# Attention and a gated two-layer network on one core: the row sums of two heads are inverted together, one head later

## The chip, the cores and the metric

One core of a Trainium2 chip. The metric is the device time of one execution in microseconds (us). Five engines work side by side, each through its own queue in order: TensorE (PE; its weight loads are listed as PEld), VectorE (DVE), ScalarE (ACT), GpSimd (POOL) and SyncE (SP), which issues most of the transfers.

## The reference

```
scores = scale * q @ k^T            # B=4, H=8, S=768, D=64
keep   = (pos_k < n_sink) | (0 <= pos_q - pos_k < window)     # 4 and 128
scores = where(keep, scores, -1e9);  scores -= rowmax
a      = exp(scores);  a = a / (sum(a) + 1e-9)
attn   = a @ v                      # then heads side by side: x is 3072 x 512
h      = x @ w_in                   # 512 x 2048
g      = max(h, 0) + log1p(exp(-|h|))
out    = g @ w_out                  # 2048 x 512
```

## The kernel before

**Tiling.** The 3072 rows are cut into 12 chunks of 256 rows, three to a batch. A chunk has 8 heads. Because of the window, a block of 128 query rows needs only its own block of keys, the block before it, and 8 keys at the start of the sequence (the sinks). So a head of a chunk is two row blocks (`j` = 0, 1) of 128 rows, each with 136 weights: 128 that hold the two key blocks folded into one square, and 8 for the sinks. From the third chunk on, products are made of a high and a low part of each number, to keep the precision; the first two chunks (`exact`) use float32 directly.

**The way of one head.** Each part is a method of `_Attention`, and a letter in the tables of `_fast`:
- `scores` (S): TensorE makes `s` in PSUM.
- `softmax` (T): VectorE folds the square and takes the row extremum (L243, L249, which also writes the negative of the scores to `a`); ScalarE takes the exponential in place and sums each row into the small tile `sm` (L250).
- `normalise` (N): VectorE adds 1e-9 to the two sums (L256) and inverts them into `rc` (L257); then the 128 weights of each row block are multiplied by it (L262 on ScalarE, L264 on VectorE or GpSimd). The string `NM` says which engine does it for the first 17 heads; for all others it is GpSimd.
- `sink_weights` and `sink` (k, K): the sinks' weights of four heads at once are multiplied by `rc` on VectorE (L269), transposed and split.
- `weights_t` (W): TensorE transposes the weights into `t` (L297); ScalarE copies them to `th`, VectorE makes the rest `tl`; GpSimd masks both into `pt` with four instructions, two of `th` and two of `tl` (L308, L311).
- `values` (V): TensorE multiplies the sinks' values (L327) and then `pt` (L333) into `x`. `out` (O) moves `x` to `xf` and splits it into `xh` (ScalarE) and `xl` (GpSimd, for the last head of a chunk VectorE).

Beside it runs the network of the chunk before (`_Moe`): `up` (U, L459), `softplus` (F, L466 to L468 on ScalarE), `gate` and `residue` (P, R: L474, `gh`, and the subtraction `gl` on VectorE), `down` (D, E: L496 to L498).

**What sets the order.** TensorE's and SyncE's instructions stand in the order in which the program calls these parts. Up to the third chunk that is the string `START`, written by hand, in which the conversion of the weights (a, c, d, l) is mixed in. From there on each step of a loop runs the letters of `STEADY` once; scores, softmax and normalise work four heads ahead of the transposition. One step per head, eight steps per chunk, and the first step of a chunk has an order of its own. At the start of a batch GpSimd also builds the sinks' values of the batch (`sinks`, L151 to L159), half of them ahead of head 6 of the chunk before. VectorE, ScalarE and GpSimd take what they are given in the order that the framework makes of the same calls, and each works through it in order.

Of the kernel before, what the change touches and what calls it, by code (L numbers as in the profile page):

```python
# [11 lines left out]
F32 = mybir.dt.float32  # L12
# [5 lines left out]
AF = mybir.ActivationFunctionType  # L18
ALU = mybir.AluOpType

B, H, S, D = 4, 8, 768, 64
DM, DFF = 512, 2048
P = 128
# [3 lines left out]
CH = 2  # L27
# [10 lines left out]
G = 4  # L38
# [24 lines left out]
def _turn(engines, k):  # L63

    return engines[min(k, len(engines) - 1)]
# [57 lines left out]
class _Attention:  # L123
# [110 lines left out]
    def softmax(self, h):  # L234
        c, nc, chunk = self.c, self.c.nc, self.chunk
        g, hh = h // G, h % G
        if hh == 0:
            self.a[g] = c.ap.tile([P, G, CH, KW], F32, tag="a", name=f"a{chunk}_{g}")
            self.rc[g] = c.sp.tile([P, CH, G], F32, tag="rc", name=f"rc{chunk}_{g}")
        sm = c.sp.tile([P, CH], F32, tag="sm", name=f"sm{chunk}_{h}")  # L240
        self.sm[h] = sm
        for j in range(CH):
            nc.vector.copy_predicated(self.s[h, j][:, :P], c.diag[:], self.s[h, j][:, KW:])  # L243
        for j in range(CH):
            a = self.a[g][:, hh, j]
            k = (chunk * H + h) * CH + j
            nm = c.stats[:, k : k + 1]
            m = c.masks[min(self.i0 + j, 2)]
            nc.vector.tensor_tensor_reduce(a, self.s.pop((h, j))[:, :KW], m[:], -SCALE, BIG, ALU.add, ALU.min, nm)  # L249
            nc.scalar.activation(a, a, AF.Exp, bias=nm, scale=-1.0, accum_out=sm[:, j : j + 1])  # L250

    def normalise(self, h):
        c, nc = self.c, self.c.nc
        g, hh = h // G, h % G
        rc, sm = self.rc[g][:, :, hh], self.sm.pop(h)
        nc.vector.tensor_scalar(sm[:], sm[:], 1e-9, None, ALU.add)  # L256
        nc.vector.reciprocal(rc, sm[:])  # L257
        for j in range(CH):
            a = self.a[g][:, hh, j, :P]
            eng = _turn(c.NM, self.chunk * H + h)  # L260
            if eng == "A":
                nc.scalar.mul(a, a, rc[:, j : j + 1])  # L262
            else:
                (nc.vector if eng == "V" else nc.gpsimd).tensor_scalar(a, a, rc[:, j : j + 1], 0.0, ALU.mult, ALU.add)  # L264

    def sink_weights(self, g):
        c, nc, chunk = self.c, self.c.nc, self.chunk
# [639 lines left out]
```

## Time and profile before

| | us |
|---|---|
| median of 3 runs | 729.31 (729.26 to 729.64) |
| the profiled execution, its own time | 731.77 |
| its span, first to last instruction | 730.1 |
| TensorE busy | 701.6 |
| VectorE busy | 579.6 |
| ScalarE busy | 452.2 |
| GpSimd busy | 377.5 |

A row of a timeline gives the start in us from the beginning of the span, the duration, the engine, the line, the instruction, what it writes and reads, and the shape; in brackets stand the idle time of the engine ahead of it and what ended it. A row of the waits gives who waited for whom, the sum, how often, and the longest.

### The profile page before, as it was taken

The numbers are of one execution on the slowest core, as the hardware profiler recorded it, in microseconds if no ns is written. First come the engines' busy times: TensorE is split into PE (matmuls) and PEld (weight loads), VectorE is DVE, ScalarE is ACT, GpSimd is POOL, SyncE is SP. The second block draws the span as 40 slices with busy tenths as digits, with TensorE's granted clock in tenths as the row PEclk, the third lists the DMA queues.
The fourth block names the chain that finished last, engine by engine and source line by source line (L and its number), as shares of the span: only waits on it lengthen the run. The fifth ranks groups of instructions, "written<-read, shape, count | busy, mean of one in ns | idle before, by whom it ended". The sixth has DMA issues, their size and how long they took to land.

```text
span 730.1 us, 13819 instructions
## 1 busy us (share of the span) xinstructions
PE 701.6 (96%) x4505; PEld 622.6 (85%) x4505; DVE 579.6 (79%) x1693; ACT 452.2 (62%) x1104; POOL 377.5 (52%) x682
## 2 busy tenths in 40 slices
PE   7789999999999999999999999999999999999996
PEld 5467789988898998989899898898898898998995
DVE  6799988878988888887987987988898887864332
ACT  4579856666765766665666666665766666654331
POOL 5666486565564554664554564556555465552000
PEclk9899999999999999999999999999999999999998
DMA  9886622211411321321222222221212222100001
GB/s 308 268 316 216 182 67 74 73 53 38 118 49 48 110 64 49 106 64 46 84 64 67 77 79 68 78 76 45 86 51 79 69 76 78 58 14 1 29 1 34
DMA packets 40875, 63.21 MB, mean 87 GB/s; under 512 B 4634, under 2 KB 22362, under 8 KB 40794
## 3 DMA queue, kind: packets, MB, share of 16 engines
q1 hardware_dynamic: 40506, 61.97, 27.9%
q8 instruction: 38, 0.62, 0.4%
q14 instruction: 43, 0.35, 0.2%
q10 hardware_dynamic: 288, 0.26, 0.1%
HBM read 55.93 MB, written 6.29 MB: 85 GB/s over the span
## 4 chain that ended last, share of the span: by engine, by line
PE 73%; DVE 8%; ACT 7%; POOL 7%; issue 4%; DMA 1%; POOLq 0%; ACTq 0%
PE h L459 30%; PE acc L498 10%; PE acc L496 9%; PE acc L497 9%; PE x L333 6%; PE t L297 2%; POOL pt L308 2%; PE s L230 2%; PE s L231 2%; PE x L327 2%; POOL pt L311 2%; ACT a L250 1%; ACT mt L466 1%; ACT mt L467 1%; POOL vs L159 1%
## 5 line engine op out<-in xcount | busy, mean ns | idle before, releaser
L459 PE MATMUL h<-xh,wi 128*128 128x256 f32 x1536 | 253.6, 287 | 0.0
L459 PEld LDWEIGHTS h<-xh,wi 128*128 128x128 f32 x1536 | 211.1, 191 | 1.6 <-issue 0.5
L264 POOL TENSOR_SCALAR a<-a,rc 128x128 f32<-128x128 f32 x178 | 69.2, 401 | 186.1 <-DVE rc L257 150.4
L459 PE MATMUL h<-xl,wi 128*128 128x256 f32 x768 | 154.5, 283 | 0.0
L496 PE MATMUL acc<-wo,gh 128*128 128x512 f32 x384 | 151.7, 395 | 0.0
L498 PE MATMUL acc<-wo,gl 128*128 128x512 f32 x384 | 150.9, 393 | 0.6 <-DVE gl L56 0.6
L497 PE MATMUL acc<-wo,gh 128*128 128x512 f32 x384 | 150.6, 392 | 0.0
L459 PEld LDWEIGHTS h<-xl,wi 128*128 128x128 f32 x768 | 119.6, 192 | 0.0
L474 DVE SCALAR_TENSOR_TENSOR mt<-h,mt 128x512 f32<-128x512 f32 x96 | 66.1, 688 | 66.8 <-ACT mt L468 58.4
L466 ACT ACTIVATE mt<-h 128x512 f32<-128x512 f32 x96 | 57.1, 595 | 96.0 <-PE h L459 96.0
L250 ACT ACTIVATE a<-a,stats 128x136 f32<-128x136 f32 x192 | 76.3, 398 | 56.9 <-DVE stats L249 56.3
L498 PEld LDWEIGHTS acc<-wo,gl 128*128 128x128 f32 x384 | 72.1, 188 | 17.5 <-DVE gl L56 1.0
L496 PEld LDWEIGHTS acc<-wo,gh 128*128 128x128 f32 x384 | 72.1, 188 | 12.8 <-issue 0.3
L497 PEld LDWEIGHTS acc<-wo,gh 128*128 128x128 f32 x384 | 72.2, 188 | 9.0
L56 DVE TENSOR_TENSOR gl<-mt,gh 128x512 fp32r<-128x512 f32 x96 | 74.8, 780 | 0.3
L308 POOL TENSOR_SCALAR_AFFINE_SELECT pt<-tl 128x256 fp32r<-128x256 f32 x80 | 59.7, 746 | 27.8 <-DVE tl L56 27.7
L308 POOL TENSOR_SCALAR_AFFINE_SELECT pt<-th 128x256 fp32r<-128x256 f32 (+1 forms) x96 | 42.5, 442 | 40.2 <-ACT th L48 36.7
L467 ACT ACTIVATE mt<-mt 128x512 f32<-128x512 f32 x96 | 60.7, 633 | 3.1
L468 ACT ACTIVATE mt<-mt 128x512 f32<-128x512 f32 x96 | 60.7, 632 | 3.0
L48 ACT CAST qkh<-qk 128x656 fp32r<-128x656 f32 x80 | 59.5, 744 | 0.9 <-DMA qk<-qk 0.9
L333 PE MATMUL x<-pt,vv 128*128 128x256 f32 (+1 forms) x216 | 48.7, 328 | 8.0 <-POOL pt L311 8.0
L56 DVE TENSOR_TENSOR kl<-qk,qkh 128x400 fp32r<-128x400 f32 x80 | 53.6, 670 | 2.5
(185 smaller groups left out, 1234.7 us busy)
## 6 DMA issues: line engine op xcount, KB each, us to landing
qk<-qk SPq DMA_DIRECT2D x160, 164.0 KB, 3.1
vr<-v SPq DMA_DIRECT2D x32, 192.0 KB, 2.8
out<-o SPq DMA_DIRECT2D x24, 256.0 KB, 2.2
vr<-v SPq DMA_DIRECT2D x16, 128.0 KB, 2.3
q<-q SPq DMA_DIRECT2D x7, 256.0 KB, 5.1
k<-k SPq DMA_DIRECT2D x8, 200.0 KB, 4.1
wi00r<-w SPq DMA_DIRECT2D x1, 511.8 KB
wi01r<-w SPq DMA_DIRECT2D x1, 511.8 KB, 6.3
```

The lines of the kernel that those rows point to most:

```text
L56: (nc.vector if eng == "V" else nc.gpsimd).tensor_tensor(out, a, b, ALU.subtract)
L250: nc.scalar.activation(a, a, AF.Exp, bias=nm, scale=-1.0, accum_out=sm[:, j : j + 1])
L264: (nc.vector if eng == "V" else nc.gpsimd).tensor_scalar(a, a, rc[:, j : j + 1], 0.0, ALU.mult, ALU.add)
L308: nc.gpsimd.affine_select(pt[:, e, :, 1], src[:], [[0, CH], [1, P]], ALU.is_ge, 0.0, base=0, channel_multiplier=-1)
L333: nc.tensor.matmul(x[:, :, o], w, pt[:, :, m], start=False, stop=n == 2, skip_group_check=True)
L459: nc.tensor.matmul(h[:, j], wt, x, start=k == 0, stop=k >= len(prods) - 2, skip_group_check=True)
L466: nc.scalar.activation(t[:], h[:], AF.Abs)
L467: nc.scalar.activation(t[:], t[:], AF.Exp, scale=-1.0)
L474: nc.vector.scalar_tensor_tensor(t[:], h[:], 0.0, t[:], ALU.max, ALU.add)
L496: nc.tensor.matmul(acc[:], gh[:, j, q], wh, start=f == 0, stop=False, skip_group_check=True)
L497: nc.tensor.matmul(acc[:], gh[:, j, q], wl, start=False, stop=False, skip_group_check=True)
L498: nc.tensor.matmul(acc[:], gl[:, j, q], wh, start=False, stop=f == 2 * FP - 1, skip_group_check=True)
```

## The change

`softmax` gives the two heads of a pair one tile of sums with four columns. `normalise` returns at once for an even head. For an odd head it adds 1e-9 to all four sums, inverts them with one instruction, and then issues the multiplications of both heads, the even one's first.

```diff
--- before.py
+++ after.py
@@ -237,8 +237,9 @@
         if hh == 0:
             self.a[g] = c.ap.tile([P, G, CH, KW], F32, tag="a", name=f"a{chunk}_{g}")
             self.rc[g] = c.sp.tile([P, CH, G], F32, tag="rc", name=f"rc{chunk}_{g}")
-        sm = c.sp.tile([P, CH], F32, tag="sm", name=f"sm{chunk}_{h}")
-        self.sm[h] = sm
+        if h % 2 == 0:
+            self.sums = c.sp.tile([P, CH, 2], F32, tag="sm", name=f"sm{chunk}_{h}")
+        self.sm[h] = sm = self.sums
         for j in range(CH):
             nc.vector.copy_predicated(self.s[h, j][:, :P], c.diag[:], self.s[h, j][:, KW:])
         for j in range(CH):
@@ -247,21 +248,26 @@
             nm = c.stats[:, k : k + 1]
             m = c.masks[min(self.i0 + j, 2)]
             nc.vector.tensor_tensor_reduce(a, self.s.pop((h, j))[:, :KW], m[:], -SCALE, BIG, ALU.add, ALU.min, nm)
-            nc.scalar.activation(a, a, AF.Exp, bias=nm, scale=-1.0, accum_out=sm[:, j : j + 1])
+            nc.scalar.activation(a, a, AF.Exp, bias=nm, scale=-1.0, accum_out=sm[:, j, h % 2 : h % 2 + 1])
 
     def normalise(self, h):
+
+        if h % 2 == 0:
+            return
         c, nc = self.c, self.c.nc
         g, hh = h // G, h % G
-        rc, sm = self.rc[g][:, :, hh], self.sm.pop(h)
+        rc, sm = self.rc[g], self.sm.pop(h)
+        assert self.sm.pop(h - 1) is sm
         nc.vector.tensor_scalar(sm[:], sm[:], 1e-9, None, ALU.add)
-        nc.vector.reciprocal(rc, sm[:])
-        for j in range(CH):
-            a = self.a[g][:, hh, j, :P]
-            eng = _turn(c.NM, self.chunk * H + h)
-            if eng == "A":
-                nc.scalar.mul(a, a, rc[:, j : j + 1])
-            else:
-                (nc.vector if eng == "V" else nc.gpsimd).tensor_scalar(a, a, rc[:, j : j + 1], 0.0, ALU.mult, ALU.add)
+        nc.vector.reciprocal(rc[:, :, hh - 1 : hh + 1], sm[:])
+        for e in (hh - 1, hh):
+            eng = _turn(c.NM, self.chunk * H + g * G + e)
+            for j in range(CH):
+                a, r = self.a[g][:, e, j, :P], rc[:, j, e : e + 1]
+                if eng == "A":
+                    nc.scalar.mul(a, a, r)
+                else:
+                    (nc.vector if eng == "V" else nc.gpsimd).tensor_scalar(a, a, r, 0.0, ALU.mult, ALU.add)
 
     def sink_weights(self, g):
         c, nc, chunk = self.c, self.c.nc, self.chunk
```

TensorE's and SyncE's instructions stand in the same order as before in the part that runs (`_general`, for other sizes, does not). On the other three engines instructions go or move.

GpSimd, late in the last chunk ahead of a new batch: `pt_5` masks head 5 of the chunk, `a_0` and `rc_0` are the weights and reciprocals of heads 0 to 3 of the next chunk, `xl` the low part of the output of heads 4 and 5, `vsh` the first of the sinks' values. Before:

```order
L264 TENSOR_SCALAR a_0_1914<-a_0_1914,rc_0_1915 128x128 x2
L308 AFFINE_SELECT pt_5_1964<-th_5_1960 128x2x128
L311 AFFINE_SELECT pt_5_1964<-th_5_1960 128x2x128
L308 AFFINE_SELECT pt_5_1964<-tl_5_1962 128x2x128
L311 AFFINE_SELECT pt_5_1964<-tl_5_1962 128x2x128
L56 TENSOR_TENSOR vv_3_1971<-vr_3_1848,vv_3_1971 128x6x64
L264 TENSOR_SCALAR a_0_1914<-a_0_1914,rc_0_1915 128x128 x2
L56 TENSOR_TENSOR xl_1534<-xf_4_1941,xh_1533 128x256
L151 TENSOR_SCALAR vsh_2053<-vsr_2051 64x128
```

And now (the line numbers behind the change are higher by 6):

```order
L314 AFFINE_SELECT pt_5_1924<-th_5_1920 128x2x128
L317 AFFINE_SELECT pt_5_1924<-th_5_1920 128x2x128
L314 AFFINE_SELECT pt_5_1924<-tl_5_1922 128x2x128
L317 AFFINE_SELECT pt_5_1924<-tl_5_1922 128x2x128
L56 TENSOR_TENSOR vv_3_1931<-vr_3_1812,vv_3_1931 128x6x64
L270 TENSOR_SCALAR a_0_1878<-a_0_1878,rc_0_1879 128x128 x4
L56 TENSOR_TENSOR xl_1500<-xf_4_1901,xh_1499 128x256
L151 TENSOR_SCALAR vsh_2014<-vsr_2012 64x128
L152 TENSOR_TENSOR vsr_2012<-vsr_2012,vsh_2014 64x128
```

The two multiplications of the even head stood ahead of `pt_5` and now stand with those of the odd head, four in a row, ahead of `xl` and `vsh`. It is the same in every odd step, with the next head's `pt` behind `xl` where no sinks' values are built.

GpSimd, in the first chunk, while the first weights `wi` are converted (`a_1` and `rc_1` belong to heads 4 to 7). Before:

```order
L56 TENSOR_TENSOR wi_335<-wt_0_0_318,wi_335 128x512
L264 TENSOR_SCALAR a_1_298<-a_1_298,rc_1_299 128x128 x2
L56 TENSOR_TENSOR wi_346<-wt_0_1_320,wi_346 128x512
L308 AFFINE_SELECT pt_2_366<-th_2_364 128x2x128
L311 AFFINE_SELECT pt_2_366<-th_2_364 128x128
L52 TENSOR_SCALAR wi_378<-wt_0_0_337 128x512
L308 AFFINE_SELECT pt_3_396<-th_3_394 128x2x128
L311 AFFINE_SELECT pt_3_396<-th_3_394 128x128
L56 TENSOR_TENSOR wi_378<-wt_0_0_337,wi_378 128x512
L264 TENSOR_SCALAR a_1_298<-a_1_298,rc_1_299 128x128 x4
```

And now:

```order
L56 TENSOR_TENSOR wi_329<-wt_0_0_312,wi_329 128x512
L56 TENSOR_TENSOR wi_339<-wt_0_1_314,wi_339 128x512
L314 AFFINE_SELECT pt_2_355<-th_2_353 128x2x128
L317 AFFINE_SELECT pt_2_355<-th_2_353 128x128
L52 TENSOR_SCALAR wi_367<-wt_0_0_331 128x512
L314 AFFINE_SELECT pt_3_385<-th_3_383 128x2x128
L317 AFFINE_SELECT pt_3_385<-th_3_383 128x128
L56 TENSOR_TENSOR wi_367<-wt_0_0_331,wi_367 128x512
L270 TENSOR_SCALAR a_1_290<-a_1_290,rc_1_291 128x128 x6
```

The two multiplications of head 4 left their place ahead of the second `wi` and stand behind the third, with those of heads 6 and 7 (head 5 is ScalarE's).

VectorE, in the second chunk (`sm_2`, `sm_3`: heads 2 and 3). Before:

```order
L50 CAST upper_183<-wo10r 128x512
L256 TENSOR_SCALAR sm_3_564<-sm_3_564 128x2
L257 RECIPROCAL rc_0_447<-sm_3_564 128x2
L256 TENSOR_SCALAR sm_2_529<-sm_2_529 128x2
L257 RECIPROCAL rc_0_447<-sm_2_529 128x2
L264 TENSOR_SCALAR a_0_446<-a_0_446,rc_0_447 128x128 x2
L269 TENSOR_TENSOR sa_0_595<-a_0_446,rc_0_447 128x64
```

And now:

```order
L50 CAST upper_183<-wo10r 128x512
L261 TENSOR_SCALAR sm_2_518<-sm_2_518 128x4
L262 RECIPROCAL rc_0_435<-sm_2_518 128x2x2
L270 TENSOR_SCALAR a_0_434<-a_0_434,rc_0_435 128x128 x2
L275 TENSOR_TENSOR sa_0_577<-a_0_434,rc_0_435 128x64
```

One addition and one reciprocal of the four are gone; the two that are left work on four numbers.

## The prediction

> **What bounds the kernel now.** I read the page first: the share of the span in which TensorE works, and its granted clock.
>
> ```profile
> span 730.1 us, 13819 instructions
> PE 701.6 (96%) x4505; PEld 622.6 (85%) x4505; DVE 579.6 (79%) x1693; ACT 452.2 (62%) x1104; POOL 377.5 (52%) x682
> ```
>
> TensorE is busy for 701.6 of 730.1 us, so the change can only act through what makes TensorE wait: 28.5 us in all. Next I asked who TensorE waited for between 108 and 640 us, which is the regular part of the program, where each step handles one head.
>
> ```profile
> PE x L333 <- POOL pt L311: 8.0, 11, 1.6
> ```
>
> That is the only wait there: 11 times, 8.0 us, and always the same one. The product with the values (L333) waits for the last masked weights `pt` from GpSimd. So in the regular part one question decides: does the change make GpSimd finish `pt` earlier or later than TensorE asks for it? The groups by line show what is removed.
>
> ```profile
> L256 DVE TENSOR_SCALAR sm<-sm 128x2 f32<-128x2 f32 x96 | 18.0, 187 | 9.9 <-ACT a L250 9.8
> L257 DVE RECIPROCAL rc<-sm 128x2 f32<-128x2 f32 x96 | 16.1, 168 | 3.3
> ```
>
> **What goes.** 96 heads have an addition of 187 ns and a reciprocal of 168 ns. 48 of each go: 48 x 0.355 = 17.0 us of VectorE. The 48 that stay work on four numbers instead of two; two more cannot be seen in 168 ns, so I take them at the same price. VectorE should fall to about 562.6 us. In the regular part I take zero for them. TensorE waits for GpSimd there, and in the step ahead of most of those waits (a chunk's first) VectorE's next instruction behind the pair that goes is this one:
>
> ```profile
> 229.05 0.69 DVE L474 SCALAR_TENSOR_TENSOR mt<-h,mt 128x512 f32<-128x512 f32 x1 [1.43 <-ACT mt L468]
> ```
>
> It stands idle for 1.43 until ScalarE is done; 0.355 less in front of it makes that 1.79. If that cover were gone, it would be up to 0.355 in each of the 8 waits that are not batch starts, 2.8 us of gain; I see nothing that takes it away.
>
> **What moves.** The multiplications by the reciprocal (L264) of an even head now stand behind those of the next odd head's reciprocals: on GpSimd four in a row in every odd step, none in an even one. The reciprocals of an odd head come at the same time as before. Behind the four stand `xl`, and then the `pt` of the next head. Three times in the program, where the next batch begins, GpSimd also builds the sink values (L151 to L159) in between:
>
> ```profile
> 149.73 0.72 POOL L264 TENSOR_SCALAR a<-a,rc 128x128 f32<-128x128 f32 x2 [1.89 <-DVE rc L257]
> 150.85 0.74 POOL L56 TENSOR_TENSOR xl<-xf,xh 128x256 fp32r<-128x256 f32 x1 [0.40 <-ACT xh L48]
> 151.57 0.29 POOL L151 TENSOR_SCALAR vsh<-vsr 64x128 fp32r<-64x128 f32 x1
> ...
> 155.98 0.58 POOL L311 TENSOR_SCALAR_AFFINE_SELECT pt<-tl 128x256 fp32r<-128x256 f32 x1
> ```
> ```profile
> 156.62 0.62 PE L333 MATMUL x<-pt,vv 128*128 128x256 f32 x2 [1.57 <-POOL pt L311]
> ...
> 498.14 0.61 PE L333 MATMUL x<-pt,vv 128*128 128x256 f32 x2 [1.57 <-POOL pt L311]
> ```
>
> Two multiplications take 0.72, so four take 1.44 and end at 151.17 instead of 150.45. `xl` used to wait 0.40 for ScalarE and start at 150.85; now it starts 0.32 later. From there to the `pt` that ends at 156.56 GpSimd has no gap, and TensorE already waits 1.57 for that `pt`. So each of the three places (the rows are the first and the last) costs its full 0.32: **3 x 0.32 = 1.0 us**. Its bounds are 0, if the stretched instructions in between take up the shift, and 3 x 0.85, if they stretch more (below).
>
> **The step behind the first odd step of each chunk.** Here `pt` arrives with almost nothing to spare. On GpSimd, VectorE, ScalarE and TensorE's weight loads:
>
> ```profile
> 236.68 0.72 POOL L264 TENSOR_SCALAR a<-a,rc 128x128 f32<-128x128 f32 x2 [1.47 <-DVE rc L257]
> 237.79 0.74 POOL L56 TENSOR_TENSOR xl<-xf,xh 128x256 fp32r<-128x256 f32 x1 [0.40 <-ACT xh L48]
> 238.67 0.41 POOL L308 TENSOR_SCALAR_AFFINE_SELECT pt<-th 128x256 fp32r<-128x256 f32 x1
> 239.03 0.41 POOL L311 TENSOR_SCALAR_AFFINE_SELECT pt<-th 128x256 fp32r<-128x256 f32 x1
> 239.38 0.86 POOL L308 TENSOR_SCALAR_AFFINE_SELECT pt<-tl 128x256 fp32r<-128x256 f32 x1
> 240.20 0.59 POOL L311 TENSOR_SCALAR_AFFINE_SELECT pt<-tl 128x256 fp32r<-128x256 f32 x1
> ```
> ```profile
> 239.04 0.94 DVE L56 TENSOR_TENSOR gl<-mt,gh 128x512 fp32r<-128x512 f32 x1
> ```
> ```profile
> 238.22 0.38 ACT L48 CAST th<-t 128x256 fp32r<-128x256 f32 x1
> ```
> ```profile
> 240.91 0.42 PEld L333 LDWEIGHTS x<-pt,vv 128*128 128x128 f32 x3
> ```
>
> `pt` ends at 240.79, its weight load starts at 240.91. Where TensorE did wait, the matmul began 0.06 after `pt` ended (156.56 to 156.62), so about 0.07 is spare. The step stands in each chunk from the fourth to the eleventh, eight times; five are like this one, and this is the last of the five:
>
> ```profile
> 582.44 0.31 PEld L333 LDWEIGHTS x<-pt,vv 128*128 128x128 f32 x2
> ```
>
> With four multiplications, which end at 238.12, `xl` ends near 238.86 instead of 238.53. The first `pt` waited for `th` (238.60), so it moves only from 238.67 to about 238.80: 0.13. That alone costs 0.13 - 0.07 = 0.06.
>
> But the four `pt` do not have fixed lengths. The third takes 0.86, twice the first, while VectorE's residue `gl` runs, a subtraction of two operands in SBUF: the two engines take turns. `gl` starts 0.01 after the second `pt`, so it gets in behind that one. With the first `pt` 0.13 later, `gl` is already waiting when the first ends. How that looks stands in another step, GpSimd and then VectorE:
>
> ```profile
> 251.65 0.41 POOL L308 TENSOR_SCALAR_AFFINE_SELECT pt<-th 128x256 fp32r<-128x256 f32 x1
> 252.01 0.86 POOL L311 TENSOR_SCALAR_AFFINE_SELECT pt<-th 128x256 fp32r<-128x256 f32 x1
> 252.83 0.59 POOL L308 TENSOR_SCALAR_AFFINE_SELECT pt<-tl 128x256 fp32r<-128x256 f32 x1
> 253.37 0.73 POOL L311 TENSOR_SCALAR_AFFINE_SELECT pt<-tl 128x256 fp32r<-128x256 f32 x1
> ```
> ```profile
> 251.72 0.88 DVE L56 TENSOR_TENSOR gl<-mt,gh 128x512 fp32r<-128x512 f32 x1
> ```
>
> Here `gl` comes 0.07 after the first `pt`, the second `pt` is the stretched one, and VectorE gets in once more before the end: 251.65 to 254.10 is 2.45 us for the four, against 2.12 from 238.67 to 240.79. So the delay is 0.13 + 0.33 - 0.07 = 0.39. In the other three, in the first chunk of a batch, two of the four are smaller:
>
> ```profile
> 182.77 0.41 POOL L308 TENSOR_SCALAR_AFFINE_SELECT pt<-th 128x256 fp32r<-128x256 f32 x1
> ...
> 184.19 0.47 POOL L311 TENSOR_SCALAR_AFFINE_SELECT pt<-tl 128x128 fp32r<-128x128 f32 x1
> ```
> ```profile
> 195.49 0.41 POOL L308 TENSOR_SCALAR_AFFINE_SELECT pt<-th 128x256 fp32r<-128x256 f32 x1
> ...
> 197.11 0.62 POOL L311 TENSOR_SCALAR_AFFINE_SELECT pt<-tl 128x128 fp32r<-128x128 f32 x1
> ```
> ```profile
> 184.87 0.31 PEld L333 LDWEIGHTS x<-pt,vv 128*128 128x128 f32 x2
> ```
>
> 1.89 us now, 2.24 in the other order, and 184.87 - 184.66 - 0.05 = 0.16 spare: 0.13 + 0.35 - 0.16 = 0.32. Together **5 x 0.39 + 3 x 0.32 = 2.9 us**. The bounds: 5 x 0.06 = 0.3 if the order of turns stays, 2.9 if it flips. I take 2.9, because 0.13 is many times the 0.01 by which the order stands now.
>
> [...]
>
> **The start.** Up to 108 us the weights are converted as well, and VectorE is at times full (2.93 of 3 us below). Some removed pairs stand on the way. VectorE, GpSimd, TensorE, then two windows (from:to, length, busy time of PE, PEld, DVE, ACT and POOL with counts, granted clock, DMA share, GB/s):
>
> ```profile
> 9.08 0.40 DVE L256 TENSOR_SCALAR sm<-sm 128x2 f32<-128x2 f32 x1 [0.74 <-ACT a L250]
> ...
> 40.10 0.15 DVE L256 TENSOR_SCALAR sm<-sm 128x2 f32<-128x2 f32 x1
> 40.29 0.17 DVE L257 RECIPROCAL rc<-sm 128x2 f32<-128x2 f32 x1
> ```
> ```profile
> 19.57 0.72 POOL L264 TENSOR_SCALAR a<-a,rc 128x128 f32<-128x128 f32 x2 [0.40 <-DVE rc L257]
> ...
> 25.21 1.57 POOL L264 TENSOR_SCALAR a<-a,rc 128x128 f32<-128x128 f32 x2
> ```
> ```profile
> 23.62 1.12 PE L327 MATMUL x<-sk,vsf 128*64 128x256 f32 x2 [3.40 <-DVE xl L56]
> ```
> ```profile
> 44.00:47.00 3.00, 0.51 (x4) 0.11 (x2) 2.93 (x11) 1.81 (x7) 1.52 (x2) 0.96 1.03 390
> 47.00:50.00 3.00, 2.78 (x9) 1.66 (x9) 2.97 (x6) 2.77 (x6) 2.41 (x3) 0.50 1.03 408
> ```
>
> At 9.08 VectorE no longer stops 0.74 for the first head's sums. At 19.57 the multiplications of head 4 leave the place in front of the work that ends in the 3.40 us wait. Around 40 us one addition and reciprocal (0.32) leave a stretch without gaps. Against this, head 4's multiplications now stand where 25.21 shows two taking 1.57, right before TensorE transposes that head. As bounds I take a gain of 0.74 + 0.72 + 0.32 = 1.8 and a loss of 1.57 - 0.72 = 0.85; for the value **-0.3**, the 0.32 of the pair around 40 us: TensorE's next long wait (44 to 47) is for what VectorE does behind it, while the gain in front of 23.62 and the loss behind it are of one size, 0.72 and 0.85.
>
> **Sum.** 1.0 + 2.9 - 0.3 = +3.6 us. The profiled execution took 731.77 us with a span of 730.1, some 2.5 above the median of the runs, 729.31; I carry the difference over: 729.31 + 3.6 = **732.9**.
>
> **The rivals.**
> - *The order of turns holds.* If GpSimd's second `pt` still gets in before `gl`, the middle term is 0.3: 1.0 + 0.3 - 0.3 = +1.0, 730.3, which is not slower by what can be told. For it: no row shows `gl` arriving in the middle of a `pt`. Against it: at 251.72 GpSimd gave way at once. It decides at a shift of a few hundredths. Chance 0.20.
> - *The shift is swallowed everywhere.* Stretched instructions between 151.57 and 155.98 may absorb the 0.32, and the order of turns holds: 0 + 0 - 0.3, 729.0. Chance 0.10.
> - *The batch starts flip too.* If the sink values there fall into a worse order of turns, each of the three costs up to 0.85 instead of 0.32: +1.6 more, 734.5. For it: the same two engines meet there. Chance 0.14.
> - *The start pays.* The windows show TensorE idle for 2.49 of 3 us and 0.22 more, and then a granted clock of 0.50 for 3 us, worth 1.5 us. If VectorE's shorter stretch ends that wait early enough, the clock stays up: -1.5, half the gain bound (-0.9), and 0.3 each for the other two terms give 727.5. Against it: some 0.3 off a wait of 2.7. Chance 0.06. [...]
>
> **How the numbers follow.** My case has 0.50, with its own range of 731.8 to 734.0. What a measurement of this kernel can tell is 0.2%, 1.46 us: 727.85 to 730.77. Slower by more: my case and the flipped batch starts, and 0.03 of the first rival: 0.67. Faster by more: most of the last, 0.05. Within: 0.28. A range of 729.5 to 735.0 leaves out the second and the last rival, 0.16, and little above.
>
> **What would show it.** In the changed profile: VectorE near 562.6 us with 1597 instructions; TensorE's waits for `pt` between 108 and 640 us at about 11.9 us and 19 times instead of 8.0 and 11; the batch starts' 1.57 at about 1.9; in the step near 239 us the second `pt` stretched instead of the third. I am wrong if those waits stay near 8.0, or if the time up to 108 us moves by more than a microsecond.

## The result and the profile after

The changed kernel takes **739.04 us** (median of 4 runs, 738.08 to 739.61); before took 729.35 beside it (729.26 to 729.64). The ratio of the runs is 1.0119, with an interval of 1.0105 to 1.0133 (the two medians alone give the upper end of it): slower, by 9.7 us between the medians, where 3.6 were predicted. The profiled execution of after took 738.08 with a span of 736.4. The page's first lines, after:

```profile
span 736.4 us, 13636 instructions
PE 706.3 (96%) x4505; PEld 624.3 (85%) x4505; DVE 570.5 (77%) x1597; ACT 452.0 (61%) x1104; POOL 377.3 (51%) x682
```

VectorE lost 9.1 us of busy time, not 17.0, though the two groups cost what was assumed (169 and 178 ns on four numbers):

```profile
L262 DVE RECIPROCAL rc<-sm 128x4 f32<-128x4 f32 x48 | 8.6, 178 | 1.6
L261 DVE TENSOR_SCALAR sm<-sm 128x4 f32<-128x4 f32 x48 | 8.1, 169 | 3.0 <-ACT a L251 3.0
```

Their durations fell by 18.0 + 16.1 - 8.6 - 8.1 = 17.4. But neighbours on VectorE overlap in the timeline (in before, below, `sa` ends at 222.68 and `tl` starts at 222.59), and an engine's busy time counts each moment once; and other groups grew (`sa` from 5.4 to 7.7, `xl` from 4.3 to 5.5).

TensorE's waits between 108 and 640 us, after:

```profile
PE x L339 <- POOL pt L317: 8.2, 11, 1.9
PE ts L287 <- DVE tl L56: 0.5, 3, 0.2
PE x L333 <- DVE sk L56: 0.4, 1, 0.4
```

Again 11 waits for `pt`, 8.2 us; there was to be 11.9 and 19. The sum hides two changes: the three at the batch starts grew from 4.7 to 5.8, the other eight fell from 3.3 to 2.4, as TensorE, held up at the chunk ends (below), comes to five of them 0.1 to 0.2 later. Two waits are new.

**Where the time went.** TensorE's order is the same in both programs, so each of its instructions can be compared with itself: how much later does it start? A second execution of before is needed for that (the first run below, span 728.0, own time 729.67), because the profiled execution that the prediction rests on, at 731.77, was not like the median one. The table gives the lag of after behind that run, and behind the execution at 731.77, at some of TensorE's products with the sinks' weights; the times are those of the first run below:

| at, us | lag of after | behind 731.77's | what lies in between |
|---|---|---|---|
| 23.8 | -0.6 | -0.4 | a little gained |
| 45.9 | 2.7 | 1.4 | waits for head 4, half clock |
| 102.3 | 4.0 | 1.5 | another stretch at half clock |
| 152.3 | 4.1 | 1.6 | |
| 161.1 | 4.4 | 2.0 | batch start: +0.36 |
| 223.8 | 5.0 | 2.5 | two chunk ends |
| 238.5 | 4.7 | 2.3 | partly given back |
| 473 | 5.6 | 3.2 | batch start, four chunk ends |
| 480 to 487 | 6.2 | 3.8 | one residue `gl` of 2.25: +0.6 |
| 502.6 | 8.2 | 5.7 | batch start +0.36, half clock +1.5 |
| 668.9 | 8.7 | 6.2 | three chunk ends |

In sums: start 4.1; three batch starts 3 x 0.36 = 1.1; half clock behind the third 1.5; one starved residue 0.6; chunk ends what is left, 1.4 (the lag grows by 0.2 to 0.3 at each of nine, and some of it is given back behind them). These are 8.7 us between two executions that took 738.08 and 729.67; the medians are 9.7 apart. Each in its rows:

*The start.* TensorE, then GpSimd, after:

```profile
25.69 0.47 PE L303 MATMUL t<-ident,a 128*128 128x128 f32 x1 [1.16 <-POOL a L270]
26.44 0.48 PE L303 MATMUL t<-ident,a 128*128 128x128 f32 x1 [0.28 <-POOL a L270]
```
```profile
24.82 1.57 POOL L270 TENSOR_SCALAR a<-a,rc 128x128 f32<-128x128 f32 x2
```

TensorE stops twice for head 4's multiplications, 1.44 us that are new. Three windows of the first run below (before) and of after (the clock is the first number behind the five engines):

```profile
24.00:28.00 4.00, 4.00 (x14) 2.39 (x14) 3.66 (x17) 3.13 (x9) 3.79 (x7) 0.65 0.90 253
28.00:32.00 4.00, 3.49 (x18) 2.18 (x17) 3.51 (x15) 2.76 (x9) 1.42 (x4) 1.00 1.02 394
49.00:53.00 4.00, 3.58 (x23) 2.65 (x22) 3.92 (x8) 3.94 (x9) 2.92 (x4) 1.00 0.43 174
```
```profile
24.00:28.00 4.00, 2.56 (x9) 1.67 (x8) 2.79 (x11) 2.69 (x9) 3.78 (x8) 0.63 0.94 298
28.00:32.00 4.00, 4.00 (x11) 2.13 (x10) 2.61 (x10) 1.38 (x6) 0.95 (x4) 0.52 0.95 385
49.00:53.00 4.00, 4.00 (x20) 3.09 (x19) 2.84 (x5) 3.83 (x8) 2.50 (x2) 0.58 1.02 410
```

Half clock comes in stretches of 3.41 us (followed through short windows). Up to 108 us before has one of them in this run and three in the profiled one; after has three, two of them in a row. They cost 1.2 to 1.5 us each: 2.4 to 2.5 for the two by which the executions of before differ, 1.3 between 45.9 and 102.3, 1.5 behind the third batch start.

*The batch starts*, after, the first and the third:

```profile
158.57 0.73 PE L339 MATMUL x<-pt,vv 128*128 128x256 f32 x3 [1.93 <-POOL pt L317]
...
502.27 0.74 PE L339 MATMUL x<-pt,vv 128*128 128x256 f32 x3 [1.92 <-POOL pt L317]
```

1.57 became 1.93, as foretold (1.9). What was not foretold follows the third one: windows of 3.4 us, before (the execution at 731.77, up to the end of the wait), then after (up to the end of the wait, and behind it):

```profile
494.70:498.10 3.40, 1.87 (x10) 1.33 (x9) 3.06 (x10) 2.55 (x7) 3.30 (x7) 1.00 0.36 93
```
```profile
498.90:502.30 3.40, 1.48 (x8) 0.97 (x6) 2.01 (x8) 2.13 (x7) 3.24 (x7) 1.00 0.36 101
502.30:505.70 3.40, 3.40 (x12) 2.68 (x12) 2.02 (x4) 0.37 (x1) 0.00 (x0) 0.59 0.00 0
```

TensorE was busy for 1.87 of 3.4 us, and in the 3.4 us behind that the clock was 1.00; now it is 1.48, and the clock behind it is 0.59.

*The chunk ends.* Here TensorE transposes the sinks' weights into `ts`, and must wait until VectorE's `tl` has read the one buffer `t`. VectorE at the end of one chunk, before (731.77) and after, then GpSimd and TensorE after:

```profile
222.12 0.43 DVE L56 TENSOR_TENSOR xl<-xf,xh 128x256 fp32r<-128x256 f32 x1 [0.47 <-ACT xh L48]
222.46 0.22 DVE L269 TENSOR_TENSOR sa<-a,rc 128x64 f32<-128x64 f32 x1
222.59 0.42 DVE L56 TENSOR_TENSOR tl<-t,th 128x256 f32<-128x256 f32 x1
```
```profile
224.30 0.57 DVE L56 TENSOR_TENSOR xl<-xf,xh 128x256 fp32r<-128x256 f32 x1 [0.47 <-ACT xh L48]
224.79 0.43 DVE L275 TENSOR_TENSOR sa<-a,rc 128x64 f32<-128x64 f32 x1
225.14 0.41 DVE L56 TENSOR_TENSOR tl<-t,th 128x256 f32<-128x256 f32 x1
```
```profile
223.17 1.43 POOL L270 TENSOR_SCALAR a<-a,rc 128x128 f32<-128x128 f32 x4 [2.17 <-DVE rc L262]
224.74 0.41 POOL L314 TENSOR_SCALAR_AFFINE_SELECT pt<-th 128x256 fp32r<-128x256 f32 x1
```
```profile
225.61 0.39 PE L287 MATMUL ts<-ident,sa 128*32 128x128 f32 x2 [0.15 <-DVE tl L56]
```

The four multiplications end at 224.60, in the middle of `xl` (0.57 for 0.43); `sa` then meets `pt` (0.43 for 0.22). `tl` starts 0.84 behind `xl` instead of 0.47.

*The starved residue.* VectorE's `gl` undisturbed, and the one at 482; then GpSimd beside the latter:

```profile
234.71 0.67 DVE L56 TENSOR_TENSOR gl<-mt,gh 128x512 fp32r<-128x512 f32 x1
...
482.29 2.25 DVE L56 TENSOR_TENSOR gl<-mt,gh 128x512 fp32r<-128x512 f32 x1
```
```profile
482.52 0.40 POOL L314 TENSOR_SCALAR_AFFINE_SELECT pt<-th 128x256 fp32r<-128x256 f32 x1
...
483.59 0.41 POOL L317 TENSOR_SCALAR_AFFINE_SELECT pt<-tl 128x256 fp32r<-128x256 f32 x1
```

All four `pt` run unstretched, one behind the other, and `gl` stands until they are done: 2.25 us for 0.67. TensorE meets it as a wait for `sk`, which VectorE makes later:

```profile
486.10 0.39 PE L333 MATMUL x<-sk,vs 128*128 128x256 f32 x1 [0.36 <-DVE sk L56]
```

Behind 108 us it happened once, and in none of the other profiles, so this 0.6 belongs to this execution.

### The profile page after: what moved, and what is told of

Its sections match the earlier page's. It is cut to its first block, busy times and chain, and to the rows that moved or that the text cites. A ratio compares the mean times of both kernels' runs of the same rounds, so it can differ in the third digit from the quotient of the medians.

```text
span 736.4 us, 13636 instructions
## 1 busy us (share of the span) xinstructions
PE 706.3 (96%) x4505; PEld 624.3 (85%) x4505; DVE 570.5 (77%) x1597; ACT 452.0 (61%) x1104; POOL 377.3 (51%) x682
## 4 chain that ended last, share of the span: by engine, by line
PE 68%; DVE 12%; ACT 8%; POOL 6%; issue 4%; DMA 1%; SPq 0%; POOLq 0%; ACTq 0%; DVEq 0%
PE h L465 28%; PE acc L504 9%; PE acc L502 9%; PE acc L503 8%; PE x L339 5%; PE t L303 2%; POOL pt L314 2%; ACT mt L473 2%; PE x L333 2%; PE s L230 2%; PE s L231 2%; ACT a L251 2%; ACT mt L472 1%; ACT mt L474 1%; POOL pt L317 1%
## 5 line engine op out<-in xcount | busy, mean ns | idle before, releaser
L314 POOL TENSOR_SCALAR_AFFINE_SELECT pt<-th 128x256 fp32r<-128x256 f32 (+1 forms) x96 | 48.9, 509 | 161.2 <-ACT th L48 155.7
L314 POOL TENSOR_SCALAR_AFFINE_SELECT pt<-tl 128x256 fp32r<-128x256 f32 x80 | 62.2, 777 | 32.1 <-DVE tl L56 31.2
```

Source lines behind the costliest of these rows:

```text
L314: nc.gpsimd.affine_select(pt[:, e, :, 1], src[:], [[0, CH], [1, P]], ALU.is_ge, 0.0, base=0, channel_multiplier=-1)
```

## The experiments

Ratios are against before, run between them on the same chip (729.81, 730.59 and 730.32 in the three groups). Edits are to the changed kernel where nothing else is said.

**1. Before again, unchanged.**

> The kernel before, unchanged, to see its spans and granted clocks run by run. The profiled execution of before took 731.77 us, its other runs 729.3; that of the changed kernel 738.08, its other runs 738.7 to 739.6 at granted clocks of 0.985 to 0.988. Theory: the difference is a number of stretches at half clock that are not the same in every execution; then the runs here near 729.3 show a clock above 0.990 and a span about 2.5 below 730.1. Rival: the profiled execution of before was only slowed as a whole; then the clock is 0.990 in all of them and the spans still differ.

730.16 (729.47 to 732.51), ratio 1.0004 (0.9993 to 1.0015). The profiled execution took 729.67 with a span of 728.0 and a mean clock of 0.997; the one that the prediction rests on had 0.990. The difference (2.1 in time, 2.4 to 2.5 at TensorE from 108 us on) is two stretches at half clock in the first 52 us, no slowing of the whole: behind 108 us the two lie a constant 2.4 to 2.5 apart. The theory holds.

**2. Pairs from the third chunk on.**

```
+        self.pair = chunk > 1                    # softmax
-        if h % 2 == 0:
+        if h % 2 == 0 and self.pair:             # normalise; without a pair as before
...
```

> Heads of the first two chunks are normalised one by one as before, pairs only from the third chunk on. Theory (sum of places: start 1.6, batch starts 1.1 and a stretch at half clock 1.5 behind the third, the sinks' weights 1.4, one long residue 0.6): the 1.6 of the start goes, 737.4, and TensorE's waits up to 108 us are those of before (3.4 for xl, 2.7 for sk). Rival: nearly all of the loss is the start and what its clock does: 730 to 731.

736.25 (733.67 to 739.54), ratio 1.0087 (1.0065 to 1.0108). Between the two theories' numbers, nearer the first: pairs in the regular part alone lose 6.4. The profile shows the three batch starts at 1.93, 1.91 and 1.93, a stretch at half clock behind the third, and a wide spread.

**3. Pairs in the first two chunks only** (the same edit with `chunk < 2`).

> The complement: pairs only in the first two chunks, heads one by one from the third chunk on. Theory: only the start is lost, 729.35 + 1.6 = 731.0, batch starts back at 1.57 and no wait behind the sinks' weights. Rival (the start is everything): 737 to 739.

734.14 (732.6 to 734.99), ratio 1.0051 (1.0037 to 1.0065): 4.3 lost in the start, where the theory had only the 1.6 of the two profiles; this one has four stretches at half clock up to 53 us, where run 1 has one. Its batch starts are 1.57 again. 6.4 + 4.3 = 10.7, against 9.7 for the whole: the two parts add up, within their spread.

**4. Moved, not merged.**

```
-        nc.vector.tensor_scalar(sm[:], sm[:], 1e-9, None, ALU.add)
-        nc.vector.reciprocal(rc[:, :, hh - 1 : hh + 1], sm[:])
+        for e in (hh - 1, hh):
+            nc.vector.tensor_scalar(sm[:, :, e % 2], sm[:, :, e % 2], 1e-9, None, ALU.add)
+            nc.vector.reciprocal(rc[:, :, e], sm[:, :, e % 2])
```

> The changed kernel with the addition and the reciprocal of each head by itself again (96 and 96 instead of 48 and 48), both at the place of the odd head: the move without the merging. Theory: the whole loss comes from the move of the multiplications, and VectorE's 9 to 17 us are worth nothing: 739 to 740. Rival: the four-number instructions on the shared tile are what costs: 730 to 733. Second rival: VectorE's saving hides part of the loss: 741 or more.

740.68 (740.43 to 741.13), ratio 1.0146 (1.0132 to 1.0159): the move alone costs all that was lost. Merging takes at most a little of it away again, 1.6 between the medians: the interval touches that of the changed kernel (1.0105 to 1.0133). TensorE's waits for `pt` are 9.3 here, 8.2 there. The time lies between the first theory and the second rival.

**5. Even heads on ScalarE** from the third chunk on.

```
             eng = _turn(c.NM, self.chunk * H + g * G + e)
+            if self.chunk > 1 and e % 2 == 0:
+                eng = "A"
```

> The changed kernel with the multiplications of every even head given to ScalarE from the third chunk on, so that GpSimd has two in a row in an odd step, as before. Theory: what the regular part lost came from the four in a row (batch starts 1.1, half clock behind them 1.5 for each stretch, the sinks' weights behind a pt 1.4, a starved residue 0.6); all of it goes and the start's loss stays: 739.0 - 4.6 = 734.4 or a little less, waits at the batch starts 1.57, the product for the sinks' weights 0.23 again. Rival: the even head's two multiplications on ScalarE stand ahead of xt and xh in its queue and move the wait there: 737 to 739.

773.28 (772.43 to 774.41), ratio 1.0582 (1.0562 to 1.0601). Both were wrong on the size; the rival had the kind. TensorE's waits for `pt` between 108 and 640 us grow from 8.2 to 18.7 and those for `ts` from 0.5 to 8.7: 18.7 of the 34 us that it takes longer than the changed kernel. Half clock follows all three batch starts here; where the rest went is open. How a wait for `pt` grows this way, run 8 shows in one place.

**6. The sinks' weights early.**

```
-Ctx.STEADY = ("kWRqpUKFSTDPNVOE", "kqWRpSDKTUFNPVEO")
+Ctx.STEADY = ("WRqpUKFSTDPNkVOE", "qWRpSDKTUFNkPVEO")     # and k one step ahead
```

> The changed kernel, with the sinks' weights (the product sa on VectorE) from the third chunk on right behind the reciprocal instead of behind xl. [...] Rival: it now meets the four multiplications and is held up there, and with it xt and xf: 739 or more.

738.72 (736.53 to 739.59), ratio 1.0102 (1.0083 to 1.0121): nothing gained. At the same chunk end `sa` takes 0.23 and `xl` 0.42, so they do escape GpSimd. But `sa` now stands ahead of `xt` and `xf`, and TensorE still loses some 0.25 there, after 0.3; and the waits for `pt` in a chunk's first step are 0.57 and 0.39 instead of 0.33 and 0.25. That the time `sa` loses at a chunk end (0.43 for 0.22) is what costs the 1.4 was my estimate, and it fell: what counts is the whole chain from the reciprocals to `tl`.

**7. Head 4 of the first chunk on ScalarE.**

```
-Ctx.NM = "PPVAPAPPPAVPPAPVP"
+Ctx.NM = "PPVAAAPPPAVPPAPVP"
```

> The changed kernel with only the multiplications of head 4 of the first chunk given to ScalarE (one letter in the table of engines). Theory: TensorE's waits of 1.16 and 0.28 for head 4 near 25.7 are what the start loses first, and the second stretch at half clock and the third follow from them: 1.6 to 4.1 less, 735 to 737.4, with the waits gone. Rival: the start loses by the later order of all of VectorE's work, not by this head: 738.5 to 739.5.

736.02 (735.03 to 737.48), ratio 1.0071 (1.0053 to 1.0088): 3.0 back for one letter. The waits of 1.16 and 0.28 are gone, and at 45.9 us TensorE is 0.0 behind run 1 instead of 2.7. What is left of the start's loss comes right behind that, a wait for `sk` of 2.79 (2.06 in run 1) with a clock of 0.68:

```profile
45.89 0.65 PE L333 MATMUL x<-sk,vsf 128*64 128x256 f32 x2 [2.79 <-ACT sk L48]
```
```profile
46.00:49.00 3.00, 3.00 (x15) 2.36 (x16) 1.87 (x3) 2.83 (x6) 1.65 (x1) 0.68 1.02 418
```

**8. Only the head at each batch start on ScalarE.**

```
+            if self.chunk in (3, 6, 9) and g * G + e == 0:
+                eng = "A"
```

> The changed kernel with only three heads changed: head 0 of the chunks that begin a batch (the fourth, seventh and tenth) is multiplied on ScalarE, so that GpSimd has two multiplications in front of the sinks' values instead of four. Theory: the three waits of 1.93 are 1.57 again, 1.1 less, and no stretch at half clock follows them, 1.5 less for each, of which an execution of the changed kernel has one or two: 735.0 to 736.4, with less spread. Rival: the stretches at half clock have nothing to do with the length of this wait: 737.9.

742.17 (740.94 to 743.32), ratio 1.0155 (1.0136 to 1.0175): slower, against both. ScalarE, GpSimd and TensorE at the first batch start:

```profile
151.03 0.70 ACT L270 ACTIVATE a<-a,rc 128x128 f32<-128x128 f32 x2 [0.72 <-DVE rc L262]
...
153.06 0.41 ACT L48 CAST xh<-xf 128x256 fp32r<-128x256 f32 x1 [0.94 <-DVE xf L360]
```
```profile
153.54 0.74 POOL L56 TENSOR_TENSOR xl<-xf,xh 128x256 fp32r<-128x256 f32 x1 [1.65 <-ACT xh L48]
```
```profile
159.31 0.73 PE L341 MATMUL x<-pt,vv 128*128 128x256 f32 x3 [2.83 <-POOL pt L319]
```

GpSimd has two multiplications again, but then waits 1.65 for `xh`: ScalarE waits 0.72 for the reciprocals, and the two multiplications stand ahead of `xt` in its queue, and so of the chain `xt`, `xf`, `xh`, `xl`. The wait grew to 2.83, and half clock follows the second and the third.

**9. The same wait shortened in another way:** `xl` on VectorE at the three batch starts.

```
-            _sub(nc, "V" if h == H - 1 else c.E["xl"], ...)
+            _sub(nc, "V" if h == H - 1 or (h == 5 and chunk in (2, 5, 8)) else c.E["xl"], ...)
```

> The changed kernel, with one subtraction moved in three places: the xl of heads 4 and 5 in the chunk ahead of each new batch is VectorE's instead of GpSimd's, so that GpSimd's chain to the awaited pt is 0.75 shorter. Theory: the three waits of 1.93 fall to about 1.2, 2.2 less, and no stretch at half clock follows them any more, 1.5 less for each of the one or two in an execution: 734.0 to 735.4. Rival: VectorE's subtraction stands ahead of tl and the wait only changes hands, 738 to 740.

734.95 (734.12 to 735.27), ratio 1.0066 (1.0053 to 1.0079): 4.1 less than the changed kernel, as the theory had it. The waits are 1.47 (I had 1.2: GpSimd's chain from `vsh` to the last `pt` takes 5.41 here for 5.15 in the changed kernel, with `vsr` at 1.01 for 0.54 beside VectorE's `gl`), and no half clock follows any of them. The shorter waits are worth 1.4 of the 4.1; between the two profiles the missing half clock is worth another 1.4, and the starved residue that did not come again 0.5.

**10. That edit on the kernel before.**

> The same edit on the kernel before: the three waits of 1.57 fall to about 0.85: 2.1 less than before on the same chip, 727.5 to 728.0 where before is at 729.6 to 730. Rival: the wait changes hands to VectorE's tl: 729 to 731.

727.51 (726.68 to 729.57), ratio **0.9967** (0.9955 to 0.9980): faster than both kernels. TensorE at the first batch start, with 0.79 for 1.57:

```profile
154.23 0.73 PE L333 MATMUL x<-pt,vv 128*128 128x256 f32 x3 [0.79 <-POOL pt L311]
```

**11. Before, with that wait made longer.**

```
-            nc.gpsimd.tensor_scalar(c.vsh[b][:], raw[:], 1.0, 0.0, ALU.mult, ALU.add)
+            for _ in range(3 if self.first else 1):
+                nc.gpsimd.tensor_scalar(c.vsh[b][:], raw[:], 1.0, 0.0, ALU.mult, ALU.add)
```

> The kernel before, in which GpSimd copies the first of the sinks' values three times instead of once at each of the three batch starts: 2 x 0.25 more in its chain, nothing else changed, no pairs. [...] Rival: the stretches at half clock in the changed kernel come from something else in the pairs: 1.5 above before with no more spread than before.

737.22 (736.19 to 737.25), ratio 1.0093 (1.0078 to 1.0107): 6.9 more, with no pair in the program, where the rival had 1.5. My own figure, 2.5 to 4.5 with a spread of 1.5 or more, was an estimate from waits of about 2.07 with one or two stretches at half clock behind them; the spread is 1.1. The copies cost 0.8, not 0.5: the waits are 2.39, 2.39 and 2.38, 2.5 us in all. The profile has half clock behind the second and third, here the third, up to the end of the wait:

```profile
497.20:500.60 3.40, 1.06 (x6) 0.61 (x4) 2.08 (x8) 1.77 (x6) 3.32 (x8) 1.00 0.34 99
```

So these stretches belong to the length of the wait, not to the pairs. Behind the first wait, as long as the others, the clock stayed at 1.00. What differs is where the wait falls. The stretches at half clock in this profile begin at 24.17, 327.95 and 502.03: whole multiples of 3.413 us apart (89 and 51). Windows laid out in that step show the first wait (152.79 to 155.18) split over two of them, and most of the third (498.26 to 500.64) in one, with half clock in the next:

```profile
150.46:153.87 3.41, 2.33 (x14) 1.79 (x13) 2.60 (x10) 2.64 (x7) 3.16 (x7) 1.00 0.36 94
153.87:157.28 3.41, 2.10 (x12) 1.76 (x12) 1.63 (x6) 0.37 (x1) 1.96 (x5) 1.00 0.04 9
498.62:502.03 3.41, 1.39 (x7) 1.22 (x8) 1.63 (x5) 0.75 (x3) 2.67 (x7) 1.00 0.18 59
502.03:505.44 3.41, 3.41 (x16) 3.01 (x15) 2.98 (x6) 1.32 (x3) 1.21 (x3) 0.50 0.00 0
```

TensorE was busy for 0.68 and 0.62 of the first two windows and for 0.41 of the third. A second wait of 1.10 behind the second batch start adds 0.8; why it grew stays open.

**12. Pairs, with the multiplications spread.** From the third chunk on; the odd head's two are issued one step later.

```
-        for e in (hh - 1, hh):
-            ...
+        self.weigh(g, hh - 1)
+        c.late.append(lambda: self.weigh(g, hh))     # called by the next, even head
...
```

> Pairs from the third chunk on (the first two chunks head by head as before), but the odd head's two multiplications wait one step more, so that GpSimd has two in every step again instead of four and none. Theory: what the regular part loses comes from the four in a row alone; batch starts 1.57, sinks' weights 0.23, no stretch at half clock behind the start, and the merging's own gain is what is left: 0 to 1 below before on the same chip. Rival: the merging itself (sums of two heads awaited, four-number instructions) costs in the regular part: 2 to 5 above before.

729.73 (728.89 to 732.58), ratio 1.0001 (0.9989 to 1.0012): all of the regular part's loss is gone, and no gain can be told. The one row of waits between 108 and 640 us is nearly that of before:

```profile
PE x L355 <- POOL pt L333: 7.9, 11, 1.6
```

## Why the prediction was wrong, point by point

The direction was right and the lever right in kind (GpSimd's four multiplications in a row), but the direction is in part luck: the largest term, 2.9, measured 0, and without it the sum would have been +0.7, which is not slower by what can be told. The whole was short by 6.1 us. The step that failed by most is the term for the start, -0.3 for 4.1. Both signs of being wrong came: the waits for `pt` stayed at 8.2, and at 102 us TensorE lies 4.0 behind run 1, 1.5 behind the execution that the prediction rests on.

- **"The change can only act through what makes TensorE wait": wrong.** Between the profile of run 1 and that of after, the span grew by 8.4, TensorE's idle time only from 28.7 to 30.1, and its busy time from 699.3 to 706.3. At half clock a product counts as busy for longer (0.63 for 0.40 us behind the third batch start), and that had no place in the sum.

- **VectorE's saving, 0 on the path: right, within what can be told.** Run 12 has 80 of the 96 instructions fewer on VectorE and stands at 1.0001. Where the multiplications stand directly behind the reciprocals the merging may be worth something (1.6 in run 4, at the edge of the noise), and there it repays part of a loss of its own. The 17.0 us were a sum of durations; of busy time it was 9.1.
- **Batch starts, +1.0: right in itself** (3 x 0.36 = 1.1, the wait at 1.93 for a predicted 1.9). The term left out what the wait does to the clock: where it falls worst, TensorE is now busy for 1.48 of 3.4 us instead of 1.85, and half clock followed one of three in the profiled execution, +1.5. The three other runs of after, 0.6 to 1.5 longer, had mean clocks of 0.985 to 0.988 against 0.990; that more such stretches made them longer is not shown, since the mean also counts half clock behind TensorE's last product (0.50 from 735.0 us on in the profiled execution, in which that product starts at 729.8). Runs 9 to 11 show that it hangs on the length of this wait (in the profiles half clock follows none of the three in runs 9 and 10, where the first is 1.47 and 0.79, and two in run 11, where it is 2.39), and run 11 on where it falls.
- **The step behind the first odd step, +2.9: wrong, it is 0.** The failing step is the shift of 0.13. GpSimd and VectorE there, after:

```profile
238.91 1.42 POOL L270 TENSOR_SCALAR a<-a,rc 128x128 f32<-128x128 f32 x4 [1.41 <-DVE rc L262]
240.30 0.75 POOL L56 TENSOR_TENSOR xl<-xf,xh 128x256 fp32r<-128x256 f32 x1
240.99 0.42 POOL L314 TENSOR_SCALAR_AFFINE_SELECT pt<-th 128x256 fp32r<-128x256 f32 x1
241.35 0.42 POOL L317 TENSOR_SCALAR_AFFINE_SELECT pt<-th 128x256 fp32r<-128x256 f32 x1
241.71 0.87 POOL L314 TENSOR_SCALAR_AFFINE_SELECT pt<-tl 128x256 fp32r<-128x256 f32 x1
```
```profile
241.34 0.97 DVE L56 TENSOR_TENSOR gl<-mt,gh 128x512 fp32r<-128x512 f32 x1
```

  With the lag of 2.30 at this place taken off, `xl` starts at 238.00, not near 238.12, and `pt` at 238.69: 0.02 later than before, not 0.13. I had started the four multiplications where the two started; they start 0.07 earlier behind the reciprocals (238.91 less 2.30 is 236.61, for 236.68). With 0.02 the order of turns held, as in the first rival: `gl` comes 0.01 ahead of the second `pt`, and the third is the stretched one, as before. An order that hangs on 0.01 was no ground for a chance of 0.50.
- **The start, -0.3 with bounds of -1.8 and +0.85: wrong, +4.1.** I saw that head 4's multiplications would stand right before TensorE's transposition, but priced them as a difference of two durations (1.57 - 0.72) against a gain in front. TensorE waits for all of what comes late: 1.16 + 0.28. The gain in front was 0.4 to 0.6, not 0.72, and came ahead of the place, where it could not pay for this. The rest, some 2.5 of the 4.1, is two more stretches at half clock than in run 1. One more letter (run 7) gives 3.0 back. And the bounds had no term for the clock, though the prediction quoted rows with 0.50.
- **The 2.5 us between the profiled execution and the median, carried over as a constant: wrong.** They were two stretches at half clock in the start (run 1), and the profile of after, its fastest run, has as many as that execution. So the start looked 2.5 cheaper to spoil than it was.
- **Not listed: the chunk ends, 1.4, and one starved residue, 0.6.** Both stand where VectorE's instructions stretch beside GpSimd's shifted ones (`xl` 0.57 for 0.43, `sa` 0.43 for 0.22, `gl` 2.25 for 0.67); I weighed only `gl` beside `pt`, and only at the places where TensorE already waited.
- **The rivals.** The order of turns did hold, as the first one said, but the sum was far from 730.3, since a loss in the start and at the clock was missing from every case. "The start pays" had the right lever, the clock, with the wrong sign.

## What to carry to other kernels

Taking work off an engine that nobody waits for was worth nothing that could be told, and what is moved to make it possible has to be costed on its own: merging two small instructions here put four multiplications in a row on the engine that TensorE waits for, while the same merging from the third chunk on with the multiplications spread cost nothing (1.0001). Cost a wait that grows twice: once for its length, and once for the clock: here 0.36 more in the third wait was followed by half clock worth another 1.5. Before summing against one profiled execution, find out in which places it differs from the median one.

## What the runs showed of the hardware

- Up to TensorE's last product, half clock (0.50) came in stretches of 3.41 us, or two in a row (6.8), in every profile. TensorE did work in the time ahead of them: 1.48 of the 3.4 us up to 502.3 in after; at before's batch starts it was 1.83 to 1.87, and no half clock followed.
- The phase can be read from the profile, since the stretches of one execution begin whole multiples of 3.413 us apart (run 11; in after those at 25.03, 48.93 and 502.90, 7 and 133 steps apart). Laid over all 14 profiles in that step, from 104 us to 685, half clock followed each of the 13 windows in which TensorE, as the profile counts it, was busy for 0.46 of the window or less, and none of the others, of which the lowest had 1.62 of 3.41 us (run 7, at 327.0). In the start the border is not so clean: 0.41 was not followed by it (run 1, at 43.9), 0.52 was (run 3, at 11.8), and so was 0.73 in a window that itself ran at half clock (after, at 25.0).
- A VectorE subtraction (`gl`, of `mt` and `gh`) stood while GpSimd ran four instructions in a row: 2.25 for 0.67, and each of the four kept its 0.40. Waiting longer did not help: `gl` is listed from 482.29, while GpSimd's `xl` ran until 482.56, and the four `pt`, from 482.52 on, all came first.
- Handing 80 small multiplications to ScalarE, an engine that was busy for 61% of the span, cost 34 us (run 5 against the changed kernel). Run 8 shows for one place that it was their place in the queue, ahead of `xt`, that counted, and not the engine's free time; for the whole 34 us that is argued.
